# Four moves at once in the first group of a fused attention, Fourier-mixing and feed-forward kernel: where weight combinations keep their temporaries, a third accumulator bank, statistics by chunk, and keys loaded ahead of values

## The chip, the cores and the metric

The kernel runs on one core of one Trainium2 chip. The metric is the device time of one launch, in microseconds (us), as the median of several runs. Before the change it was 1323.78 us (three runs, 1320.86 to 1325.08). A difference under 2% counts as "the same".

## The reference

Eight batches of 576 tokens, 8 heads of 64. Efficient attention (queries softmaxed along the head, keys along the sequence, k-transpose times v first), then a two-dimensional Fourier mix whose real part is added, a normalisation, and a feed-forward layer of 512 to 2048 to 512:

```python
q_s = softmax(q, axis=-1); k_s = softmax(k, axis=sequence)
x   = q_s @ (k_s^T @ v)                       # per head, then heads side by side
u   = x + real(fft(fft(x, axis=sequence), axis=model))
un  = (u - mean(u)) / sqrt(var(u) + 1e-6)
out = u + max(un @ w_ch1, 0) @ w_ch2          # w_ch1: 512 x 2048, w_ch2: 2048 x 512
```

## The kernel before

Each batch is a group. Group 0 takes the weights as they are ("plain": 16 blocks of the first layer, then the second layer). From group 1 on both layers run as a seven-product (Strassen) scheme with weights combined in advance. The combinations are made once, beside group 0's second layer: eight combinations for the first weight (layer 0) and eight for the second (layer 1), each of four additions that GpSimd and VectorE share. The sums go into temporaries, from there by stores to device memory (w1s, w2s), and come back as loads, numbered 15, 16, ... for group 1.

```python
# the tile "words" and the tile "unT" (normalised rows, transposed) share one buffer: same tag, bufs=1
self.words = self.work.tile([P, 7, 2, HD], F32, tag="unT", name="words", bufs=1)
unT        = self.work.tile([P, 7, 2, HD], F32, tag="unT", name="unT", bufs=1)

def combine(self, layer, p):
    w = self.w2sb if layer else self.w1sb
    t = [self.words[:, 4 + (2 * (NP * layer + p) + i) % 3] for i in range(2)]   # three places in turn
    ...                                                          # four additions into t
    nc.sync.dma_start(to[:, first], one)                         # two stores straight from w
    nc.sync.dma_start(to[:, second], two)
    for i in range(2):
        nc.sync.dma_start(to[:, 3 + 2 * i:5 + 2 * i], t[i])      # two stores of temporaries

def up(f):                                                       # a block of group 0's first layer
    n = ("ba", "bb")[f % 2]                                      # two accumulator banks
    ph = self.ps.tile([P, 512], F32, tag=n, name=n)
    ...                                                          # four matmuls into ph
    nc.scalar.activation(h[:, f, :], ph[:], ACT.Relu)            # gives the bank back

# main loop, group 0, beside the second layer
combine = [lambda l=l, p=p: blk.combine(l, p) for l in range(2) for p in range(NP)]
combine[NP:NP] = [lambda i=i: blk.load(15 + i) for i in range(4)]
side += norm(1)
merged(down, mixed(side, combine))
```

The words tile also receives the last three pieces of the second weight ("the fetch of the last pieces"), and since it shares unT's buffer it does not exist before the first layer has read unT for the last time. A scheduler orders the instructions of every engine when the program is built, by what it thinks is ready; the program's text gives priorities, not the order. And in the built program every transfer is issued by SyncE in order, and each waits for the one eight before it to have landed, because eight completion counters are used in turn.

## Time and profile before

| stage of the profiled run (TensorE) | us |
|---|---|
| start to first query transposes | 27.72 |
| to the first block of the first layer | 58.99 |
| first layer of group 0, 16 blocks | 72.42 |
| second layer, with attention and mixing of group 1 between | 91.91 |
| hole: to VectorE's first addition for group 1's products | 29.13 |
| from there to the end | 1039.1 |

The stage borders are start times of rows of the timeline: the first transposes of queries, the first matmul of the first layer (L608 before, L617 after), the first of the second layer (L617, L626), the end of its last, and VectorE's first addition into the tile u (L647, L656). The lines behind this table stand in the prediction. A row reads: start, duration, engine, source line, operation, output<-inputs, form, count, and in brackets the idle time before it and who ended it.

### The profile page before, as it was taken

To read this page: it belongs to the slowest core of one execution; us is meant where nothing else is said; L and a number is where in the kernel's file an instruction comes from. 1 tells how busy PE (TensorE), PEld (TensorE's weight loads), DVE (VectorE), ACT (ScalarE), POOL (GpSimd) and SP (SyncE) were. 2 spreads that over 40 slices of the span, in tenths; PEclk is the share of its full clock that TensorE was granted. 3 is DMA by queue.
4 is the path that set the end of the run, shared out by engine and by line. 5 is a ranking of instruction groups with operands and counts; after the bars stand their busy time and mean duration, and the time that the engine had idled before them with its cause. 6 is when DMAs were issued, how large, how long until landed. Compare 5 with 4: busy or idle time off the path is not lost.

```text
span 1319.3 us, 14360 instructions
## 1 busy us (share of the span) xinstructions
PE 1215.1 (92%) x5484; PEld 949.4 (72%) x5484; DVE 541.7 (41%) x1143; ACT 320.6 (24%) x585; POOL 380.3 (29%) x317
## 2 busy tenths in 40 slices
PE   6858999679999989998999899999999999999797
PEld 4433354368778767887788778877788778888686
DVE  5877272566332551447134613371334143202211
ACT  3555231034111420134113311241124101201100
POOL 2554252133401350016302630253023301421230
PEclk9779999889999999999999999999999999999899
DMA  8446363355225532354335432642353325353342
GB/s 257 140 156 237 117 219 116 122 173 182 111 92 155 192 128 96 126 197 148 130 130 170 170 128 92 201 179 100 116 183 119 117 92 165 142 188 121 148 183 63
DMA packets 90964, 194.52 MB, mean 147 GB/s; under 512 B 22736, under 2 KB 56272, under 8 KB 83728
## 3 DMA queue, kind: packets, MB, share of 16 engines
q1 hardware_dynamic: 89288, 192.82, 42.3%
q8 instruction: 43, 0.70, 0.2%
q10 hardware_dynamic: 1608, 0.79, 0.2%
q14 instruction: 25, 0.20, 0.0%
HBM read 168.94 MB, written 28.84 MB: 150 GB/s over the span
## 4 chain that ended last, share of the span: by engine, by line
PE 68%; DVE 5%; POOL 3%; DMA 1%; issue 1%; ACT 1%; POOLq 0%; DVEq 0%
PE bb L715 13%; PE bb L679 11%; PE bc L715 9%; PE ba L715 8%; PE ba L679 7%; PE bc L679 6%; PE acc L493 4%; PE acc L377 2%; PE acc L518 1%; PE tr L580 1%; PE acc L515 1%; DMA big<-w1s 1%; PE tr L364 1%; POOL q L409 1%; DVE qrec L412 1%
## 5 line engine op out<-in xcount | busy, mean ns | idle before, releaser
L679 PE MATMUL bb<-unT,big 128*128 128x256 f32 x768 | 191.8, 390 | 20.6 <-DVE u L647 15.7
L679 PEld LDWEIGHTS bb<-unT,big 128*128 128x128 f32 x768 | 145.9, 194 | 48.0 <-DVE u L647 18.9
L715 PE MATMUL bb<-big 128*128 128x256 f32 x768 | 177.1, 381 | 0.0
L715 PEld LDWEIGHTS bb<-big 128*128 128x128 f32 x768 | 143.4, 190 | 25.4 <-issue 6.7
L679 PE MATMUL ba<-unT,big 128*128 128x256 f32 x512 | 127.7, 389 | 7.8 <-DMA big<-w1s 7.8
L679 PE MATMUL bc<-unT,big 128*128 128x256 f32 x512 | 125.5, 382 | 0.0
L265 POOL TENSOR_TENSOR big<-big 128x512 f32<-128x512 f32 x32 | 40.5, 1267 | 274.5 <-ACT big L691 274.5
L715 PE MATMUL bc<-big 128*128 128x256 f32 x512 | 117.8, 382 | 0.5 <-DVE x L738 0.5
L715 PE MATMUL ba<-big 128*128 128x256 f32 x512 | 113.7, 379 | 0.0
L679 PEld LDWEIGHTS ba<-unT,big 128*128 128x128 f32 x512 | 97.3, 195 | 21.9 <-issue 8.7
L715 PEld LDWEIGHTS bc<-big 128*128 128x128 f32 x512 | 95.1, 190 | 17.8 <-issue 5.1
L715 PEld LDWEIGHTS ba<-big 128*128 128x128 f32 x512 | 97.1, 190 | 13.9 <-issue 0.8
L679 PEld LDWEIGHTS bc<-unT,big 128*128 128x128 f32 x512 | 94.4, 190 | 13.9 <-DVE big L690 1.3
L691 ACT ACTIVATE big<-big 128x512 f32<-128x512 f32 x96 | 60.4, 630 | 162.9 <-DVE big L690 162.8
L733 POOL TENSOR_TENSOR x<-x,u 128x512 f32<-128x512 f32 x14 | 17.9, 1281 | 230.8 <-DVE u L651 154.5
L493 PE MATMUL acc<-ft,eo 128*128 128x289 f32 (+3 forms) x240 | 76.5, 442 | 1.6 <-POOL eo L477 1.6
L647 DVE TENSOR_TENSOR u<-bb,s 128x512 f32<-128x512 f32 x40 | 27.6, 689 | 102.7 <-PE bb L679 68.4
L493 PEld LDWEIGHTS acc<-ft,eo 128*128 128x128 f32 (+3 forms) x240 | 37.6, 173 | 34.1 <-issue 24.8
L617 PE MATMUL bc<-big 128*128 128x512 f32 x128 | 60.0, 610 | 0.8 <-DVE x L622 0.8
L499 DVE COPY ZT<-acc 128x31 f32<-128x31 f32 x32 | 6.1, 190 | 131.3 <-ACT Z L498 131.3
L259 POOL TENSOR_TENSOR big<-big 128x512 int32<-128x512 int32 x27 | 42.2, 1572 | 52.6 <-DVE big L255 27.5
L690 DVE TENSOR_TENSOR big<-bc,u 128x512 f32<-128x512 f32 x64 | 44.1, 689 | 23.9 <-PE bc L679 23.0
(172 smaller groups left out, 1639.1 us busy)
## 6 DMA issues: line engine op xcount, KB each, us to landing
big<-w1s SPq DMA_DIRECT2D x64, 896.0 KB
big<-w2s SPq DMA_DIRECT2D x56, 1024.0 KB
big<-in_w_dram SPq DMA_DIRECT2D x29, 512.0 KB
k<-in_kT_dram SPq DMA_DIRECT2D x28, 288.0 KB
v<-in_v_dram SPq DMA_DIRECT2D x28, 256.0 KB
q<-in_q_dram SPq DMA_DIRECT2D x28, 256.0 KB
w1s<-words SPq DMA_DIRECT2D x16, 256.0 KB
w2s<-words SPq DMA_DIRECT2D x16, 256.0 KB
```

The source lines that it names most:

```text
L259: nc.gpsimd.tensor_tensor(out=out.bitcast(I32), in0=ti, in1=lo, op=ALU.add)
L265: e1.tensor_tensor(out=to(4), in0=at(2), in1=at(3), op=ALU.add)
L364: nc.tensor.transpose(pt[:, c, :], k[:, c * P:(c + 1) * P], self.ident[:])
L377: nc.tensor.matmul(pk, lhsT=ks[0:n, c, :], rhs=v[0:n, c, :], start=(c == 0), stop=(c == NC - 1))
L493: nc.tensor.matmul(pz, lhsT=eo[c][int(odds)][s, cols], rhs=self.ft[s, 3 * int(odds) + c, :], start=(c == 0), stop=(c == 2 and odds))
L617: nc.tensor.matmul(po[:], lhsT=h[:, f, i * P:(i + 1) * P], rhs=self.w2sb[:, f, :], start=(f == 0), stop=(f == NF - 1))
L647: V.tensor_tensor(out=temp("u2"), in0=box["bb"][:], in1=box["s1"][:], op=ALU.add)
L679: nc.tensor.matmul(bank()[:, i, :], lhsT=w[:, WA_AT[m], k * P:(k + 1) * P], rhs=unT[:, B_AT[m], k, :], start=first and i == 0 and k == 0, ...
L690: V.tensor_tensor(out=hp(i), in0=bank[:], in1=u[:], op=ALU.add)
L691: nc.scalar.activation(hp(i), hp(i), ACT.Relu)
L715: nc.tensor.matmul(bank()[:, i, :], lhsT=h[p][:, A_AT[m], i * P:(i + 1) * P], rhs=w[:, p, :], start=first and i == 0 and p == 0, stop=p == ...
L733: nc.gpsimd.tensor_tensor(out=x, in0=x, in1=t[:, c], op=ALU.add)
```

## The change

Its intent: the combinations' temporaries leave the words tile, so that group 1's unT need not wait for their stores; the other three parts shorten group 0. Source lines move by 6 to 9 (L608 becomes L617, L610 L619, L617 L626, L584 L591, L679 L688).

```diff
@@ first @@
-            if r == 0:
+            if r == 1:
                 load(v ...)                       # values after the second key tile, not the first
@@ combine @@
-        t = [self.words[:, 4 + (2 * (NP * layer + p) + i) % 3] for i in range(2)]
+        pairs = lambda a: a.rearrange("p (s n) -> p s n", s=2)
+        temp = lambda n: self.work.tile([P, 2, HD], F32, tag=n, name=n, bufs=1)[:]
+        if layer == 0 and p > 1:
+            t = [pairs(self.w1sb[:, p - 2 + NP * i, :]) for i in range(2)]
+        elif layer == 0:
+            t = [temp("s1"), temp("u2")] if p == 0 else [temp("u3"), pairs(self.halves()[:, 0:D])]
+        else:
+            t = [pairs(self.w1sb[:, NP + 2 * (p % 2) + i, :]) for i in range(2)]
@@ norm, cut: statistics and square roots of group 0 for chunks (0, 2), then (1, 3) @@
-            for i in range(4):
-                stats(i)
-            scales()
+            for some in ((0, 2), (1, 3)) if g == 0 else (range(4),):
+                for i in some:
+                    stats(i)
+                scales(slice(some[0], 4, some[1] - some[0]))
-        return unT, [all_stats] + pipelined(range(4), [normal, turn]) + [combine]
+        return unT, [all_stats] + pipelined((0, 2, 1, 3), [normal, turn]) + [combine]
@@ plain.up @@
-            n = ("ba", "bb")[f % 2]
+            n = ("ba", "bb", "bc")[f % 3]
@@ main loop @@
-            combine[NP:NP] = [lambda i=i: blk.load(15 + i) for i in range(4)]
+            combine[NP:NP] = [lambda i=i: blk.load(15 + i) for i in range(3)]
+            combine.append(lambda: blk.load(18))
```

More of the change, by code (lines that the diff above doesn't have):

```diff
@@ L565, in stats, with scales @@
             V.bn_aggr(mv[:, i, :], st[:])
-        def scales():
-            nc.scalar.activation(std[:], mv[:, :, 1], ACT.Sqrt, bias=self.eps[:, 0:1])
-            V.reciprocal(std[:], std[:])
+        def scales(s):
+            nc.scalar.activation(std[:, s], mv[:, s, 1], ACT.Sqrt, bias=self.eps[:, 0:1])
+            V.reciprocal(std[:, s], std[:, s])
         def normal(i):
```

## The prediction

> **What bounds the kernel now.** I read the page first: one core, TensorE busy for 92% of the span, so only time in which TensorE stands still or runs at a lower clock can be won. Then the table of stretches of 20 us, to find where that is.
>
> ```profile
> PE 1215.1 (92%) x5484; PEld 949.4 (72%) x5484; DVE 541.7 (41%) x1143; ACT 320.6 (24%) x585; POOL 380.3 (29%) x317
> ```
>
> In the stretches the columns are the stretch, then busy time of TensorE, its weight loads, VectorE, ScalarE, GpSimd, then clock, DMA share, GB/s:
>
> ```profile
> 80.00:100.00 20.00, 14.66 (x37) 7.66 (x38) 12.86 (x26) 8.05 (x13) 15.02 (x8) 0.77 0.57 194
> ...
> 220.00:240.00 20.00, 20.00 (x61) 9.77 (x60) 7.67 (x23) 3.13 (x6) 0.73 (x1) 1.00 0.19 66
> 240.00:260.00 20.00, 11.04 (x32) 4.96 (x30) 8.96 (x23) 0.30 (x1) 2.13 (x3) 0.83 0.32 108
> 260.00:280.00 20.00, 8.23 (x32) 6.52 (x32) 11.28 (x25) 6.88 (x12) 7.01 (x6) 0.66 0.67 200
> ```
>
> From 160 to 250 us TensorE is nearly full, and after 282 us too (longer stretches, from weights to weights, show 90 to 100% busy up to 1204 us). The losses lie before 160 and between 251 and 282. The chain of the page is no help for them: it goes back only to 277 us. So I took the timelines of single engines. The hole in the middle, on TensorE and then on ScalarE:
>
> ```profile
> 247.44 3.60 PE L617 MATMUL bc<-big 128*128 128x512 f32 x8
> 270.47 1.97 PE L580 MATMUL tr<-ident,eo 128*128 128x128 f32 x8 [19.43 <-ACT unT L584]
> 272.23 2.63 PE L679 MATMUL ba<-unT,big 128*128 128x256 f32 x8
> ```
>
> ```profile
> 269.83 1.07 ACT L584 COPY unT<-tr 128x512 f32<-128x512 f32 x2 [3.29 <-DMA w2s<-words]
> ```
>
> TensorE transposes the normalised rows of group 1 and ScalarE copies them to unT. unT shares its one buffer with words, in which the weight combinations keep their temporaries until their stores have landed. The list of waits of 158 to 300 us says the same from the other side:
>
> ```profile
> POOL words L273 <- DMA w2s<-words: 48.0, 3, 30.2
> ...
> PE tr L580 <- ACT unT L584: 19.4, 1, 19.4
> ```
>
> Three temporaries in rotation mean that every combination waits for stores of the one before. Seven of the eight of the second layer were unfinished when VectorE came to an addition that stands before them and waits for TensorE's output until 251.08 us; then they came at one per some 2.4 us, up to 267.3 us. That chain, and not work, is the hole.
>
> Before 160 us the first layer of group 0 (L608) is the place, on TensorE, with ScalarE's line that ends the last stall below it:
>
> ```profile
> 86.71 3.70 PE L608 MATMUL ba<-unT,big 128*128 128x512 f32 x8 [0.68 <-ACT unT L584]
> ...
> 96.23 5.36 PE L608 MATMUL ba<-unT,big 128*128 128x512 f32 x8 [2.39 <-ACT big L610]
> ...
> 119.81 5.37 PE L608 MATMUL bb<-unT,big 128*128 128x512 f32 x8 [2.82 <-ACT big L610]
> 126.82 3.67 PE L608 MATMUL ba<-unT,big 128*128 128x512 f32 x8 [1.64 <-POOL big L259]
> ...
> 143.62 5.37 PE L608 MATMUL ba<-unT,big 128*128 128x512 f32 x8 [2.84 <-ACT big L610]
> ```
>
> ```profile
> 141.78 0.66 ACT L250 ACTIVATE big<-big 128x512 f32<-128x512 f32 x1 [7.22 <-DMA big<-in_w_dram]
> 142.91 0.57 ACT L610 ACTIVATE big<-ba 128x512 f32<-128x512 f32 x1
> ```
>
> A block of the first layer starts every 3.44 us when nothing waits; 16 are 55.0 us, but they took 86.71 to 159.13 = 72.4 us. The banks ba and bb are given back by a Relu (L610) that stands on ScalarE behind conversions of the second weight, and those wait for that weight's loads. The start of the kernel has a wait of its own, on VectorE:
>
> ```profile
> 9.32 0.75 DVE L350 TENSOR_REDUCE km<-big 128x1 f32<-128x576 f32 x1 [3.04 <-DMA big<-in_kT_dram]
> ```
>
> **What the Trainium skill says.** "Perfetto Trace Analysis", section "Optimization Strategy": find the gaps of the contended engine, and which semaphore ends each. That is the reading above. "TensorE: Matmul & The Clock Gate", section "Part 1: The HAM clock gate": the array runs at half clock after some 3.4 us of idleness until it has been busy as long. The trace agrees in kind: a block after a stall took 5.36 us instead of 3.60, the eight passes after the hole 2.63 instead of 1.89, and both stretches show a clock under 1. So a removed stall returns somewhat more than itself. "SBUF — State Buffer", section "Who interferes with whom": GpSimd and VectorE share ports, and a VectorE operation in a two-port mode (tensor_scalar) shuts GpSimd out while it lasts. The trace has a GpSimd addition L259 that took 6.44 us at 84.99, under unbroken VectorE work, against 1.28 elsewhere; this matters for the combinations that move forward. "DMA: Bandwidth & Descriptors", section "Issuing engines are not separate DMA queues": all transfers run on the same 16 engines. So stores moved forward compete with the weight loads; DMA share there is 0.57 to 0.65 (80 to 140 us), which leaves room.
>
> **The change part by part.** The order of instructions in the built changed program tells more than the diff.
>
> (1) Temporaries in places of weights done with. No combination touches words any more; only three loaded pieces of weights do, and their last conversion ends near 177 us. In the built order the combinations of layer 1 (first) move up among the conversions, those of the second all stand before the last output addition, and group 1's statistics, normalisation and copies wait for none. Now the new time line. TensorE ends its second layer at 251.04; one transpose block moves ahead of that (+0.44), one stays behind it (0.44, and about 0.2 latency). Then the first products of group 1. Up to the product at 284.53 there are five groups of eight passes at 1.73: 8.65. So that product starts at 251.04 + 0.44 + 0.44 + 0.2 + 8.65 = 260.8, plus about 0.5 for the wait on the four additions that combine unT (0.69 on VectorE, 1.72 on GpSimd, started after the last copy): 261.3. Gain 284.53 - 261.3 = **23.2 us**, clock loss included. The load put last (18) is issued after the last output addition, near 252.5; 896 KB land some 5 us later by the rate of 200 to 250 GB/s in the windows. It is needed by the second pair, after 262. Hidden.
>
> (2) Keys ahead of values. Key tile 1 (288 KB) lands about 4 us earlier (1.15 MB of values at the 243 GB/s of the first 20 us are no longer ahead of it), and the values land when it did at the latest. But the copy L368 of the first keys' last rows now stands behind the third keys' maximum, which still comes near 10.2, so the first key-value product ends near 12.2, the second starts near 13.9 instead of 16.23. I take **2.2 us**, carried through a start that is bound by this chain.
>
> (3) Statistics by chunk. On VectorE the first reciprocal no longer stands behind two conversion steps (0.41 + 1.28 + 1.41), so normalising starts 2.5 us earlier. ScalarE's copies, however, still come behind the conversion of the second weight's first piece, which lands at 80.8 (relative to the old start). Copies then run 81.5 to 84.3 instead of 83.4 to 86.7: **2.3 us**. The price: conversions of first weights 9 to 15 move behind the normalising, VectorE is then busy without a gap, GpSimd is shut out for longer, and the loads of the second weight that wait for its additions come some 4 us later.
>
> (4) Three banks. Each block waits for the Relu of three blocks before. What sets the end of this layer is the Relu of block 10 at 142.91, behind the load of piece 13. It released block 12; now it releases 13. One block less behind it: **3.4 us**. Parts (2) and (3) reach the end only through the time of this Relu. I follow the chain of pieces 8 to 13 (load 3.4 us, conversion, GpSimd, next load 4.2 us) with the inserted combinations, and get 141.8, so 1.1 us from both together, not 4.5. Layer ends near 154.6 instead of 159.1: **4.5 us** for (2) to (4).
>
> Against it: the 16 stores of temporaries of layer 1 (256 KB each; after 160 us before) now run before about 155, and load 15 (896 KB, 4 us) stands ahead of the last three pieces of weights. The third key tile of group 1 and the last weights come later than TensorE wants them: **-1 us**.
>
> Sum: 23.2 + 4.5 - 1 = 26.7. 1323.8 - 26.7 = **1297.1 us**. From group 1 on the engines' orders are the same in both programs, so nothing else should move.
>
> **Rivals.** First: the unT wait gives way to another. Combinations still wait for stores, now in two alternating pairs of places, and these waits sit in order on VectorE and GpSimd in front of key copies and additions which TensorE needs. For: the old GpSimd waits of 30 us. Against: between 205 and 250 there is little that TensorE needs from GpSimd, and the built order leaves only the end of the last combination after 210. It would give back 5 to 10: 1302 to 1307. Second: the first layer is bound by the loads and conversions of the second weight, whatever the banks. Then (2) to (4) bring nothing or, by the crowd on GpSimd, lose 3: 1301 to 1304. For: every stall there ends with a conversion or a load. Third: stalls of the first layer vanish more fully than I count, with their slow blocks (three times 1.77): then 6 more, 1291.
>
> **Range and chances.** The 23.2 are nearly sure, give or take 1.5; the 3.5 of the rest may be -3 to +9. I give 1290 to 1304. Two per cent is 1297.3, on top of my value, so faster and same are about even: faster 0.5, same 0.49, slower 0.01.
>
> **What would show it.** No TensorE gap over 2 us near 250, and group 1's first product starts within 1.5 us of the end of the second layer; no wait of ScalarE's unT copies on a store. Second key maximum before 6 us. First-layer block 0 starts near 82, the layer ends near 154 to 155, with one stall before block 13. The prediction is wrong if a wait on stores shows up in 160 to 250 on TensorE, if load 18 holds up the second pair, or if the first layer ends at 159 again.

## The result, and the profile after

The changed kernel took 1303.94 us in the median of four runs (1298.75 to 1304.36), beside 1322.32 us for the kernel before (four runs). The ratio is 0.985, with a 95% interval of 0.982 to 0.988, which counts as the same at the limit of 2%. Ratios here are the mean time of one kernel's runs over that of the other's of the same rounds, so they are not quite the ratios of the medians that are quoted. The time lies at the upper end of the predicted range (1290 to 1304), 6.8 us above the predicted 1297.1.

The page after, busy time of each engine, shows the same work in a shorter span (1302.0 us in place of 1319.3):

```profile
PE 1213.9 (93%) x5484; PEld 949.6 (73%) x5484; DVE 542.4 (42%) x1144; ACT 320.5 (25%) x586; POOL 383.4 (29%) x317
```

In the stretches of 20 us (columns as in the prediction), TensorE is now full on both sides of 260, and at full clock:

```profile
80.00:100.00 20.00, 16.62 (x44) 7.66 (x42) 13.40 (x28) 5.98 (x11) 19.10 (x10) 0.94 0.49 153
240.00:260.00 20.00, 20.00 (x70) 11.34 (x69) 11.07 (x26) 6.40 (x10) 1.71 (x1) 1.00 0.34 105
260.00:280.00 20.00, 20.00 (x108) 17.63 (x107) 16.56 (x40) 8.55 (x18) 8.98 (x7) 1.00 0.74 250
```

The hole is gone from TensorE's timeline: the last product of the second layer, the last transposes, and group 1's first product follow each other without a bracket.

```profile
251.78 3.60 PE L626 MATMUL bc<-big 128*128 128x512 f32 x8
255.22 0.60 PE L587 MATMUL tr<-ident,eo 128*128 128x128 f32 x4
255.65 1.89 PE L688 MATMUL ba<-unT,big 128*128 128x256 f32 x8
```

But the second layer ends 4.3 us later than before, 255.38 for 251.04. The first layer starts 3.2 us earlier and ends only 0.8 earlier, and its stalls are longer than they were:

```profile
83.52 3.70 PE L617 MATMUL ba<-unT,big 128*128 128x512 f32 x8 [0.68 <-ACT unT L591]
...
102.66 5.37 PE L617 MATMUL bb<-unT,big 128*128 128x512 f32 x8 [4.28 <-ACT big L619]
...
126.56 5.37 PE L617 MATMUL ba<-unT,big 128*128 128x512 f32 x8 [4.80 <-POOL big L265]
...
142.80 5.37 PE L617 MATMUL ba<-unT,big 128*128 128x512 f32 x8 [3.71 <-ACT big L619]
...
158.30 7.03 PE L626 MATMUL bc<-big 128*128 128x512 f32 x16
...
173.18 2.79 PE L384 MATMUL acc<-v,ks 128*128 128x128 f32 x10 [6.44 <-ACT ks L372]
```

The name POOL L265 in the second bracket gives a hint, and no more than that: the view names the releaser that came last. In the built program this block waits for the Relu (L619) of block 6 and for an old conversion, not for L265; that Relu ended at 126.41, 0.03 us before the addition that the bracket names. But L265 is the first addition of a combination of the first weight, and that it runs inside the first layer is new. Its rows between 80 and 200 us, before and then after (source line, count, shortest/median/longest ns, first to last start):

```profile
L265 POOL TENSOR_TENSOR words<-big x8: 723/758/914, 159.4 to 190.5; 128x256 f32<-128x256 f32 x8
```

```profile
L265 POOL TENSOR_TENSOR big<-big x6: 732/902/1183, 106.2 to 151.6; 128x256 f32<-128x256 f32 x6
L265 POOL TENSOR_TENSOR u<-big x1: 1057/1057/1057, 89.9 to 89.9; 128x256 f32<-128x256 f32 x1
```

Before, no combination could start ahead of 159.4, since their place did not exist until the first layer had ended. After, seven of the eight run in the middle of that layer, and the first just ahead of it, at 76.26. There they share GpSimd with the additions that finish the second weight's conversion (L259) and with the subtraction of the query maxima (L416), and VectorE with the rest of the conversion: in the first layer GpSimd is busy for 49.2 us instead of 31.0, VectorE for 53.9 instead of 36.9. ScalarE, which works in order, waits for that subtraction, and its Relu, which gives the bank back, waits behind it, here before the second stall and before the third:

```profile
122.13 0.63 ACT L417 ACTIVATE q<-q 128x512 f32<-128x512 f32 x1 [7.13 <-POOL q L416]
...
125.83 0.58 ACT L619 ACTIVATE big<-ba 128x512 f32<-128x512 f32 x1
...
141.54 0.63 ACT L417 ACTIVATE q<-q 128x512 f32<-128x512 f32 x1 [6.27 <-POOL q L416]
142.07 0.58 ACT L619 ACTIVATE big<-ba 128x512 f32<-128x512 f32 x1
```

The last of these, at 142.07, starts close to where the prediction put the one that matters (141.8), 0.84 us before its forerunner at 142.91. But it is block 9's and releases block 12 at 142.80, where the prediction had block 10's releasing 13: the layer is one block behind. It falls behind at this very Relu. In e2_no_temps (below), which has the same three banks and no combinations here, block 11 starts at 134.74 and block 12, without a wait, at 138.17; here they start at 135.41 and 142.80. (The first two stalls are another matter: before 102.66 ScalarE waits for loads of the second weight, and block 9 waits in e2_no_temps too, 5.12 us, to start at 125.13.)

The second place is the start of the second layer. The fetch of the last pieces, SyncE's issues before and after:

```profile
159.32 0.81 SPq L236 DMA_DIRECT2D words<-in_w_dram  x2
```

```profile
162.89 0.33 SPq L314 DMA_DIRECT2D big<-w1s  x1
163.32 0.85 SPq L236 DMA_DIRECT2D words<-in_w_dram  x2
```

Before, it was issued 0.2 us after the first layer's end; now it stands 5.0 us behind it, in order behind stores of combinations and load 15. SyncE stands for 3.9 of these 5.0 us in front of load 15 (L314), until a store of the first weight's combinations has landed. The first piece also lands later after its issue, 6.6 us instead of 3.8. The first conversion of these pieces on ScalarE, before and after:

```profile
163.08 0.67 ACT L250 ACTIVATE big<-words 128x512 f32<-128x512 f32 x1 [3.16 <-DMA words<-in_w_dram]
```

```profile
169.95 0.66 ACT L250 ACTIVATE big<-words 128x512 f32<-128x512 f32 x1 [10.85 <-DMA words<-in_w_dram]
```

The Trainium skill, "Perfetto Trace Analysis", section "Tensor Engine Instruction (MATMUL, LD_WEIGHTS)", says that ScalarE, VectorE and GpSimd are "strict FIFO". The trace agrees: the copy of keys L372, ready long before, stands on ScalarE behind that conversion, and TensorE waits 6.44 us for it at 173.18.

By stages, the profiled runs (all in us; every row adds up to its span):

| kernel | start | to layer 1 | first layer | second layer | hole | to the end | span |
|---|---|---|---|---|---|---|---|
| before | 27.72 | 58.99 | 72.42 | 91.91 | 29.13 | 1039.1 | 1319.3 |
| after | 26.79 | 56.73 | 74.78 | 97.08 | 4.67 | 1042.0 | 1302.0 |
| difference | -0.9 | -2.3 | +2.4 | +5.2 | -24.5 | +2.9 | -17.3 |

### The profile page after: what moved, and what is told of

It is laid out like the page before. It is cut to its first block, busy times and chain, and to the rows that moved or that the text cites. A ratio compares the mean times of both kernels' runs of the same rounds, so it can differ in the third digit from the quotient of the medians.

```text
span 1302.0 us, 14354 instructions
## 1 busy us (share of the span) xinstructions
PE 1213.9 (93%) x5484; PEld 949.6 (73%) x5484; DVE 542.4 (42%) x1144; ACT 320.5 (25%) x586; POOL 383.4 (29%) x317
## 4 chain that ended last, share of the span: by engine, by line
PE 74%; DVE 4%; DMA 4%; POOL 3%; issue 1%; ACT 1%; SPq 0%; POOLq 0%; DVEq 0%; ACTq 0%
PE bb L724 13%; PE bb L688 11%; PE bc L724 9%; PE ba L724 9%; PE ba L688 7%; PE bc L688 7%; PE acc L500 4%; PE bc L626 3%; PE acc L384 3%; DMA q<-in_q_dram 2%; DMA big<-w1s 1%; PE acc L525 1%; PE tr L587 1%; PE acc L522 1%; PE tr L371 1%
## 5 line engine op out<-in xcount | busy, mean ns | idle before, releaser
L688 PE MATMUL bb<-unT,big 128*128 128x256 f32 x768 | 192.7, 391 | 18.9 <-DVE u L656 14.7
L688 PEld LDWEIGHTS bb<-unT,big 128*128 128x128 f32 x768 | 146.6, 195 | 46.1 <-DVE u L656 19.5
L724 PEld LDWEIGHTS bb<-big 128*128 128x128 f32 x768 | 143.4, 190 | 25.4 <-issue 6.7
L688 PE MATMUL ba<-unT,big 128*128 128x256 f32 x512 | 127.6, 388 | 7.6 <-DMA big<-w1s 7.6
L688 PE MATMUL bc<-unT,big 128*128 128x256 f32 x512 | 125.2, 381 | 0.0
L265 POOL TENSOR_TENSOR big<-big 128x512 f32<-128x512 f32 (+1 forms) x38 | 46.0, 1211 | 268.3 <-ACT big L700 262.8
L688 PEld LDWEIGHTS ba<-unT,big 128*128 128x128 f32 x512 | 97.3, 195 | 21.9 <-issue 8.6
L724 PEld LDWEIGHTS bc<-big 128*128 128x128 f32 x512 | 95.1, 190 | 17.8 <-issue 5.1
L688 PEld LDWEIGHTS bc<-unT,big 128*128 128x128 f32 x512 | 94.6, 190 | 13.1 <-DVE big L699 0.6
L656 DVE TENSOR_TENSOR u<-bb,s 128x512 f32<-128x512 f32 x40 | 27.6, 689 | 101.6 <-PE bb L688 67.3
L273 POOL TENSOR_TENSOR unT<-unT 128x512 f32<-128x512 f32 x8 | 14.2, 1770 | 180.6 <-DVE unT L272 180.6
L626 PE MATMUL bc<-big 128*128 128x512 f32 x128 | 58.9, 600 | 0.3 <-DVE x L631 0.3
L259 POOL TENSOR_TENSOR big<-big 128x512 int32<-128x512 int32 x27 | 45.0, 1674 | 41.2 <-DVE big L255 21.5
```

Of the source, the lines that this page charges most:

```text
L259: nc.gpsimd.tensor_tensor(out=out.bitcast(I32), in0=ti, in1=lo, op=ALU.add)
L265: e1.tensor_tensor(out=to(4), in0=at(2), in1=at(3), op=ALU.add)
L273: e2.tensor_tensor(out=to(1), in0=at(3), in1=at(1), op=ALU.subtract)
L626: nc.tensor.matmul(po[:], lhsT=h[:, f, i * P:(i + 1) * P], rhs=self.w2sb[:, f, :], start=(f == 0), stop=(f == NF - 1))
L656: V.tensor_tensor(out=temp("u2"), in0=box["bb"][:], in1=box["s1"][:], op=ALU.add)
L688: nc.tensor.matmul(bank()[:, i, :], lhsT=w[:, WA_AT[m], k * P:(k + 1) * P], rhs=unT[:, B_AT[m], k, :], start=first and i == 0 and k == 0, ...
```

## The experiments

Twelve kernels were run, in five rounds each, with the kernel before beside them on the same chip. The stage table of their profiled runs, in the order told below:

| label | what it is | start | to layer 1 | first layer | second layer | hole | to the end | median (runs) | ratio to before, 95% |
|---|---|---|---|---|---|---|---|---|---|
| e1_only_temps | temporaries alone | 25.40 | 61.79 | 74.35 | 97.25 | 5.00 | 1039.7 | 1306.65 (4) | 0.9876 (0.9856 to 0.9897) |
| e2_no_temps | the other three alone | 27.38 | 57.03 | 69.41 | 91.80 | 29.22 | 1040.4 | 1316.69 (6) | 0.9950 (0.9931 to 0.9969) |
| e3_load15_late | whole, load 15 late | 23.85 | 57.05 | 74.32 | 98.65 | 4.67 | 1043.5 | 1303.80 (5) | 0.9855 (0.9833 to 0.9878) |
| e4_stats_whole | whole, statistics as before | 26.38 | 60.21 | 72.69 | 99.62 | 5.00 | 1041.2 | 1306.64 (6) | 0.9873 (0.9849 to 0.9898) |
| e5_second_temps_all | whole, first weight's temporaries back | 24.42 | 57.43 | 68.99 | 93.67 | 6.17 | 1056.9 | 1309.44 (6) | 0.9912 (0.9886 to 0.9939) |
| e6_second_temps_only | only the second weight's moved | 27.04 | 59.35 | 71.98 | 93.63 | 6.18 | 1054.4 | 1316.47 (6) | 0.9967 (0.9939 to 0.9996) |
| e7_two_banks | whole, two banks | 24.48 | 56.92 | 79.35 | 95.13 | 4.67 | 1041.4 | 1300.28 (6) | 0.9851 (0.9823 to 0.9878) |
| e8_values_first | whole, values first | 23.61 | 56.96 | 74.57 | 96.88 | 4.67 | 1041.0 | 1303.57 (6) | 0.9871 (0.9841 to 0.9902) |
| e9_held_and_spread | combinations held back, then all at once | 27.00 | 58.42 | 68.53 | 101.56 | 5.53 | 1043.5 | 1304.41 (4) | 0.9874 (0.9859 to 0.9889) |
| e10_whole_again | the change, unchanged | 24.54 | 58.60 | 74.23 | 96.78 | 4.66 | 1040.5 | 1302.85 (4) | 0.9867 (0.9849 to 0.9886) |
| e11_paced | held back and paced | 26.17 | 57.19 | 68.99 | 99.49 | 4.66 | 1044.8 | 1303.27 (6) | 0.9852 (0.9824 to 0.9881) |
| e12_paced_four | the same, four pairs of places | 24.19 | 57.16 | 69.05 | 99.89 | 9.16 | 1042.2 | 1309.10 (6) | 0.9910 (0.9876 to 0.9943) |

### The temporaries alone (e1_only_temps)

The `combine` and main-loop hunks of the change, applied to the kernel before; nothing else.

> The kernel before with the first part of the change alone: the temporaries of the combinations out of the tile of the last weight pieces, and load 18 behind the combinations. Theory A (the traces' reading: this part carries all of the gain; the first layer's end came only 0.8 us earlier, so the other three parts are worth 0 to 1 us): the median is that of the whole change, 1303 to 1305 us against about 1322, and group 1's first product follows the last product of group 0 within 1.5 us. Theory B (the prediction's sum with one term mis-sized: the three small parts do bring 4.5 us, and the loss of 4.5 us behind load 15 eats it): without them it is 1307 to 1309. Theory C (the three small parts do harm, because the unbroken VectorE work of the new order starves GpSimd at 81 us and delays the loads of the second weight): 1300 to 1302. In all three the words fetch stands behind load 15 as in the whole change, so the TensorE stall before the second k times v of group 1 is there, 5 to 7 us.

It took 1306.65 us, between theories A and B. The stages say more than the sum: the hole shrinks from 29.13 to 5.00 us, a gain of 24.1, and at the same time the first layer is 1.9 us longer and the second 5.3 us longer than before. So the first part brings its gain whole and pays for it in both layers by itself.

### The other three parts alone (e2_no_temps)

```diff
-        t = [... pairs(self.w1sb ...) ...]
+        t = [self.words[:, 4 + (2 * (NP * layer + p) + i) % 3] for i in range(2)]
-            combine[NP:NP] = [... for i in range(3)]; combine.append(lambda: blk.load(18))
+            combine[NP:NP] = [lambda i=i: blk.load(15 + i) for i in range(4)]
```

> The changed kernel with the first part undone: temporaries back in the tile of the last weight pieces, load 18 back; keys first, chunk statistics and three banks stay. Theory A: 1321 to 1323, as before, with the hole of some 24 us before group 1 there again, and the first layer's end within 1 us of the kernel before's. Theory B: 1317 to 1318. Theory C: 1323 to 1326. If the hole is set by store landings that do not move with the first layer's end, small gains in the first layer vanish in the hole and all theories give 1321 to 1323; then the trace's first-layer end decides: 158 to 159 for A, 154 to 156 for B, later than 159 for C.

It took 1316.69 us, 5.9 less than the kernel before, and its first layer ends at 153.82:

```profile
84.41 6.24 PE L610 MATMUL ba<-unT,big 128*128 128x512 f32 x8 [0.68 <-ACT unT L584]
...
138.17 3.60 PE L610 MATMUL ba<-unT,big 128*128 128x512 f32 x8
143.44 3.67 PE L610 MATMUL bb<-unT,big 128*128 128x512 f32 x8 [1.67 <-ACT big L612]
...
265.34 1.97 PE L580 MATMUL tr<-ident,eo 128*128 128x128 f32 x8 [19.72 <-ACT unT L584]
```

That is close to theory B, and theory A (the three small parts bring 0 to 1) falls. The first layer took 69.41 us instead of 72.42, and its end moved by 5.3 us, where the prediction had 4.5. The hole stays (19.72 us of wait on TensorE, 29.22 to the first addition), and it moved along with the layers rather than swallowing their gain. Alone, then, the three small parts do what was predicted, and the temporaries bring their gain at the hole but cost some 7 us in the two layers. In the first layer the halves also cost each other: -3.0 us for the small parts and +1.9 for the temporaries would make 71.3 us, and together it is 74.78.

### Load 15 out of the way (e3_load15_late)

```diff
-            combine[NP:NP] = [lambda i=i: blk.load(15 + i) for i in range(3)]
-            combine.append(lambda: blk.load(18))
+            combine[NP:NP] = [lambda i=i: blk.load(15 + i) for i in range(1, 3)]
+            combine += [lambda i=i: blk.load(i) for i in (15, 18)]
```

> The whole change, and load 15 issued with load 18 behind all combinations. Theory A on the second layer (the 4.5 us lost there come because load 15, 896 KB, waits on SP for the last store of the first layer's temporaries and the fetch of the last weight pieces stands behind it in order and shares its bandwidth): the fetch issues at 159 to 160 instead of 163.3, the stall of TensorE before the second k times v shrinks from 6.4 us to under 3, group 1 starts 3 to 5 us earlier, and the end is 1299 to 1301 us. Rival: the second layer is held by the engines' chain of conversions and key copies or by the clock, whatever the fetch: 1303 to 1305, with a stall of 5 to 7 us still. Second rival: load 15, issued near 240, lands too late or pushes the stores and key loads of group 2: later than 1305, with a wait for a load of the weights at group 1's first product.

A miss: 1303.80 us, a second layer of 98.65. The fetch was issued 5.3 us after the first layer's end (155.22), as late as in the changed kernel (5.0), and the stall was there:

```profile
160.54 0.97 SPq L236 DMA_DIRECT2D words<-in_w_dram  x2
```

```profile
169.21 2.08 PE L384 MATMUL acc<-v,ks 128*128 128x128 f32 x8 [5.55 <-ACT ks L372]
```

With load 15 gone, stores of the second weight's combinations moved up in the built order and took its place: ten issues of w2s stores stand ahead of the fetch, the last held until 159.80, where the changed kernel has seven. Load 15 by itself is not the cause; what stood in its place did the same.

### Statistics in one piece again (e4_stats_whole)

```diff
-            for some in ((0, 2), (1, 3)) if g == 0 else (range(4),):
+            for some in (range(4),):
-        ... pipelined((0, 2, 1, 3), [normal, turn]) ...
+        ... pipelined(range(4), [normal, turn]) ...
```

> The whole change with the statistics of group 0 in one piece again and the normalising in the old order 0, 1, 2, 3 (the third part undone alone). Theory A: 1303 to 1305; the first layer starts some 2 us later than 83.5 and ends at 158 to 160. Theory B (the part is worth its 2.3 us): 1305.5 to 1307. Theory C (the part starves GpSimd and delays the loads of the second weight by some us): 1300 to 1302.5, with the seven loads of the second weight issued at 80 to 86 us instead of 89.8 and the waits of ScalarE for them near 93 gone.

It took 1306.64 us, 2.7 to 3.8 more than the two medians of the whole change, as theory B has it. But its runs spread from 1302.25 to 1311.62, and its ratio to the kernel before (0.9873) lies within the intervals of both (0.985 and 0.9867), so the times do not decide. The stage in question, from the query transposes to the first layer, is 60.21 us here and 61.79 with the temporaries alone, which also lacks this part; over the four profiles without chunk statistics it is 59.0 to 61.8 (mean 60.1), over the ten with them 56.7 to 58.6 (mean 57.3). So the part brings 2 to 3 us there. Counted from the start of the kernel, the first layer begins at 86.4 to 87.2 us in the four, whose starts took 25.4 to 27.7, and at 80.6 to 85.4 in the ten, mostly in the order of their starts (23.6 to 27.4): in these profiles a quick start reaches the layer only with this part.

### Only the second weight's temporaries moved (e5_second_temps_all, e6_second_temps_only)

```diff
-        if layer == 0 and p > 1: ...
-        elif layer == 0: ...
+        if layer == 0:
+            t = [self.words[:, 4 + (2 * p + i) % 3] for i in range(2)]
         else:
             t = [pairs(self.w1sb[:, NP + 2 * (p % 2) + i, :]) for i in range(2)]
```

The first applies this to the changed kernel, the second to the kernel before (with load 18 behind the combinations).

> The whole change, but the combinations of the first weight keep their temporaries in the tile of the last weight pieces, as before; only those of the second weight go to places of weights done with. Theory A (what the whole change lost came from the first weight's combinations: freed from that tile, they run inside the first layer on GpSimd and VectorE and their stores stand ahead of the fetch of the last weight pieces; the hole before group 1 was due to the second weight's temporaries alone): the first layer ends at 153 to 155 us as without the first part, the fetch issues within 1 us of it, the second layer takes some 92 us, no wait for a store before group 1's unT copy, group 1's first product at 246 to 249, and the end at 1293 to 1297 us. Rival (the stores of the first weight's combinations alone still hold unT past 250): a hole of 5 us or more stays, 1299 to 1304. Second rival (the loss in the second layer has another cause, such as load 15 and the key loads): second layer 96 or more, 1298 to 1301.

> The kernel before, with nothing but the temporaries of the second weight's combinations moved (and load 18 behind the combinations). Theory A: the first layer ends at 159 as before, the second layer takes some 92 us, the hole of some 24 us goes: 1297 to 1301 us, which is faster than the first part whole alone (1306.65) by 6 to 9 us. Rivals: 1304 to 1308 if the loss has another cause than where the first weight's combinations run.

Up to group 1 theory A is right in every stage: first layer 68.99 and 71.98 us (as without the first part), second layer 93.67 and 93.63, and the hole gone, 6.2 us. In e5_second_temps_all the first addition of group 1 came at 250.68, 9.4 us before that of the changed kernel. The times are nevertheless misses, 1309.44 and 1316.47, because the stretch from there to the end took 1056.9 and 1054.4 us instead of some 1041. In e5_second_temps_all SyncE is held up by stores that stand in front of group 2's keys, and TensorE then waits for the keys. (The first row merges four issues: the second went out at 250.45, 24.5 us after the first.)

```profile
225.50 27.04 SPq L301 DMA_DIRECT2D w2s<-big  x4
```

```profile
269.77 1.12 PE L368 MATMUL tr<-ident,k 128*128 128x128 f32 x4 [8.53 <-ACT k L357]
```

These stores wait for additions of the second weight's combinations, which the scheduler had now put behind group 1's normalising (GpSimd idles from 199.1 to 246.4 and makes them from 248.1 on). The keys, which follow in order, were issued at 264.21; in the changed kernel at 239.83. The gain was made and handed back 20 us later: with the shorter waits that follow, TensorE stands for 12.2 us between 261 and 300 us. e6_second_temps_only shows the same wait for keys, 8.33 us.

### Two banks, and values first (e7_two_banks, e8_values_first)

```diff
-            n = ("ba", "bb", "bc")[f % 3]
+            n = ("ba", "bb")[f % 2]
```

```diff
-            if r == 1:
+            if r == 0:
```

> The whole change with two banks in the first layer again. Theory A (with the first weight's combinations inside the first layer, the Relu copies come late because ScalarE waits behind conversions and q exponentials that wait for GpSimd and VectorE; a third bank lets TensorE run ahead through some of it): the first layer takes 1 to 3 us longer than 74.8, end 1305 to 1307. Prediction's size for the part (3.4 us): 1307 to 1308. Rival (the banks no longer matter): 1303 to 1304.5.

> The whole change with the values loaded after the first key tile again. Theory A (the start gained 0.9 us at the q transposes instead of 2.2, because the third key tile came 1.1 us later): 1304 to 1305. Prediction's size with all of it reaching the end: 1306. Rival (it gains nothing): 1303 to 1304. Runs of one kernel spread by some 5 us, so only a difference of 2 us or more will be read from the times; otherwise the trace's second key maximum (4.6 against 9.3 us) and q transposes (26.8 against 27.7) decide.

With two banks the first layer takes 79.35 us, 4.6 more than the changed kernel's 74.78, but the second layer is 2 us shorter (95.13), and the timed runs do not show the difference: a median of 1300.28, below that of the whole change and below all that was expected, with a ratio (0.9851) like that of the change (0.985). What the third bank is worth in the layer is shown; that it is worth anything at the end, beside these temporaries, is not.

Values first took 1303.57 us, between the two medians of the whole change, and its start was the shortest of all profiles (23.61 us). A start is best compared at one clock: where all the products of keys and values ran slowly, it took 27.04 and 27.72 us with values first (e6_second_temps_only, before) and 26.79, 27.00 and 27.38 with keys first (after, e9_held_and_spread, e2_no_temps). Loading keys ahead of values brings nothing that these runs can show.

### Combinations held back until the layer is over (e9_held_and_spread), and the change again (e10_whole_again)

```diff
-            t = [temp("s1"), temp("u2")] if p == 0 else [temp("u3"), pairs(self.halves()[:, 0:D])]
+            t = [self.words[:, 4], self.words[:, 5]] if p == 0 else [self.words[:, 6], temp("u3")]
-            t = [pairs(self.w1sb[:, NP + 2 * (p % 2) + i, :]) for i in range(2)]
+            t = [pairs(self.w1sb[:, (12 + 2 * p) % NF + i, :]) for i in range(2)]
-            combine[NP:NP] = [... for i in range(3)]; combine.append(lambda: blk.load(18))
+            combine += [lambda i=i: blk.load(15 + i) for i in range(4)]
```

> The whole change with three edits that follow from the runs so far. The first two combinations of the first weight take their temporaries from the tile of the last weight pieces (and u3), which is not free before the first layer ends, so that the combinations after them, which write over places whose stores come later, cannot start inside the first layer. The combinations of the second weight take eight different pairs of places, all of the first weight's, so that none of them waits for another's store. The four loads for group 1 follow all combinations. Theory A (the two losses of the whole change come from the first weight's combinations running inside the first layer and standing ahead of the fetch; the loss of the run with only the second weight's temporaries moved came from its late stores ahead of group 2's key loads): first layer 69 to 70 us, second layer 92 to 95, under 1.5 us to the first product, from there to the end 1040 to 1043: 1292 to 1296 us, 0.978 to 0.981 of before. Rival (the loss of that run after group 1's start has another cause and stays): 1304 to 1310. Second rival (the loads for group 1, now behind 16 more stores, come late): a wait of TensorE for a weight load at group 1's first products, 1297 to 1303.

> The changed kernel again, unchanged, on the same chip as the run above: how far its stages repeat. Expected: 1301 to 1305 us; first layer 74 to 76 us and second layer 96 to 98 in its profile, as the first time; the time up to the first q transposes somewhere in 23.5 to 27.5 us (the profiles so far fall on 23.6 to 24.5 or on 25.4 to 27.7 whatever the kernel) and the stretch from group 1's first addition to the end somewhere in 1039 to 1044. If these two vary while the edits stand still, a loss of 2.9 us in that stretch is none of the change's.

The held version does for the first layer what theory A says, 68.53 us, and the fetch goes out 0.2 us after its end:

```profile
154.14 0.81 SPq L236 DMA_DIRECT2D words<-in_w_dram  x2
```

```profile
173.41 0.79 PE L384 MATMUL acc<-v,ks 64*128 64x128 f32 x2 [10.13 <-DVE ks L375]
```

Still it is a miss, 1304.41 us. With places enough for all of them, the eight combinations follow each other without a pause from 154.19 on, and VectorE works through fifteen of their additions and two conversions before it comes to L375, the copy of the first keys' last rows, at 173.08. TensorE waits 10.13 us for that. VectorE's additions are slower here, too: beside GpSimd's additions most of them take 0.93 to 0.95 us, against 0.41 when GpSimd stands still (172.14). The stretch to the end (1043.5) did not show the late keys again. So an early fetch by itself does not give the short second layer; what else the two engines have in front of them counts as well.

The whole change run again took 1302.85 us. Its layers repeat within 0.6 us (74.23 and 96.78), and the two stretches that were to be watched vary: 24.54 against 26.79 us at the start, 1040.5 against 1042.0 to the end. The start differs mostly because the same rows of ten products of keys and values ran at different speeds, on TensorE in the first profile of the change and then in the second:

```profile
19.50 2.80 PE L384 MATMUL acc<-big,ks 128*128 128x128 f32 x10 [0.52 <-ACT ks L372]
```

```profile
20.15 1.57 PE L384 MATMUL acc<-big,ks 128*128 128x128 f32 x10 [0.52 <-ACT ks L372]
```

The Trainium skill, "TensorE: Matmul & The Clock Gate", section "Part 1: The HAM clock gate", says that the window in which activity is judged is free-running, so that the same kernel leaves the slow clock after a different number of matmuls from run to run. The trace agrees: 2.80 and 1.57 us for the same row.

### Paced (e11_paced, e12_paced_four)

Both keep the first weight's temporaries in the words tile, three places in turn, as in e5_second_temps_all. The second weight's get sixteen different places in the first and four pairs in turn in the second, and loads follow later.

```diff
 # e11_paced, against e5_second_temps_all
-            t = [pairs(self.w1sb[:, NP + 2 * (p % 2) + i, :]) for i in range(2)]
+            t = [pairs(self.w1sb[:, p + NP * i, :]) for i in range(2)]
-            combine[NP:NP] = [... for i in range(3)]; combine.append(lambda: blk.load(18))
+            combine += [lambda i=i: blk.load(15 + i) for i in range(4)]
 # e12_paced_four, against e5_second_temps_all
-            t = [pairs(self.w1sb[:, NP + 2 * (p % 2) + i, :]) for i in range(2)]
+            t = [pairs(self.w1sb[:, NP // 2 + 2 * (p % 4) + i, :]) for i in range(2)]
-            combine[NP:NP] = [... for i in range(3)]; combine.append(lambda: blk.load(18))
+            combine[NP:NP] = [lambda i=i: blk.load(15 + i) for i in range(2)]
+            combine += [lambda i=i: blk.load(i) for i in (17, 18)]
-            side += norm(1)
-            merged(down, mixed(side, combine))
+            merged(down, mixed(side, combine) + norm(1))
```

> The whole change, with the first weight's combinations in the tile of the last weight pieces as in the run of 1309 us (three places there, so that each waits for the stores of one before: they are paced), and those of the second weight in sixteen different places, each in the two that its namesake of the first weight has been read from and stored; the four loads for group 1 follow all combinations. Theory A (what cost the held-back version its 10 us was eight combinations at once on VectorE and GpSimd ahead of the copy of keys; what cost the version with only the second weight's temporaries moved its 15 us was their late run, after the normalising, with group 2's keys behind their stores): first layer 68 to 70 us, second layer 92 to 95, first product within 1.5 us, from group 1's first addition to the end 1040 to 1044: 1291 to 1296 us, 0.977 to 0.981 of before. Rival (work on VectorE and GpSimd beside the first key tiles costs the second layer wherever it comes from): second layer 97 to 101, 1297 to 1303. Second rival (the stores end so late that group 2's keys are late again): 1303 or more.

> The paced version again (first weight's combinations in the tile of the last weight pieces), but the second weight's use four pairs of places in turn instead of eight, so that in the built order the last ones move behind group 1's query work, one of them behind the normalising; and the normalising follows all combinations in program order. Theory A (the paced version's second layer of 99.5 us instead of 93.7 comes from the second weight's combinations on VectorE and GpSimd beside the key and query chains): second layer 94 to 97, first layer 69, group 1's first product within 1.5 us, from group 1's first addition to the end 1040 to 1046 with a wait of up to 4 us for keys if the last combination's stores hold them: 1294 to 1300 us. Rival (the loss in the second layer is due to stores and loads on the queue, not to the engines): 98 to 100, 1301 to 1305. Second rival (the one late combination brings back the late keys): the stretch to the end 1048 or more, 1303 to 1309.

The first layer is 69.0 us in both, as expected; the second is 99.49 and 99.89 instead of 92 to 97. In e11_paced TensorE waits for 6.9 us in the second layer (2.7 before), by the sum of the brackets in its timeline, and has a mean granted clock of 0.95 there instead of 0.98; its own work takes 92.6 us instead of 89.2. The hole does not come back in the first (4.66), and the late keys do not either, but the stretch to the end is the longest of the versions without them (1044.8). At 1303.27 us it is as fast as the changed kernel and no faster. e12_paced_four is inconclusive: its six runs spread from 1303.08 to 1317.62, the profile belongs to one of the fastest, and it has 9.16 us of the hole again. Neither beats the changed kernel, and no version tried beats it by more than the spread of the runs.

## Why the prediction was right or wrong

The range held the time by 0.06 us at its upper end, while its middle value was 6.8 us off. That it held at all is luck in part, since the losses in the two layers could as well have come out a little larger. One of its own signs of being wrong nearly came true: the first layer ended at 158.30, where it had named 159. The steps fared differently.

**The hole, 23.2 us: right.** From the end of the second layer to group 1's first addition the change took 24.5 us away, and 24.1 by itself. The product that started at 284.53 starts at 264.52; it was predicted for 261.3, and the 3.2 us between are more than made up of the later end of the second layer (255.38 for 251.04, where the prediction had 251.04 unchanged in this step). No copy to unT waits for a store any more. One reading beside it was too generous: the slow blocks that the prediction shows for the clock followed stalls of 2.39 to 2.84 us, shorter than the 3.4 us that it quotes, so these rows do not confirm that figure.

**Keys ahead of values, 2.2 us: wrong.** The second key maximum came at 4.63 us, before 6 as predicted, but the third, which the working took to stay near 10.2, came at 11.28, behind a landing:

```profile
4.63 0.74 DVE L357 TENSOR_REDUCE km<-big 128x1 f32<-128x576 f32 x1
...
11.28 0.75 DVE L357 TENSOR_REDUCE km<-big 128x1 f32<-128x576 f32 x1 [4.16 <-DMA big<-in_kT_dram]
```

The copy L375 waits behind it, as the working said it would, and now a microsecond later. The start gained 0.9 us in the first profile; with the part undone it was shorter still. What the start varies by, 23.6 to 27.7 us over all profiles, is for the most part the speed of these products: each of the last two rows of ten took either 1.57 or 2.80 us, up to 2.5 us in all. The rest goes with when the first keys and values landed.

**Statistics by chunk, 2.3 us: right in kind and size** (2 to 3 us before the first layer). The price that the prediction named was paid too: under unbroken VectorE work one GpSimd addition that takes 1.28 us elsewhere took seven times as long, and the seven loads of the second weight behind it were issued from 89.84 on. Before, two of them went out at 80.52 and five from 91.46 on, so only the first two were late:

```profile
80.82 8.99 POOL L259 TENSOR_TENSOR big<-big 128x512 int32<-128x512 int32 x1 [2.90 <-ACT eo L250]
```

**Three banks, 3.4 us, and 4.5 us for (2) to (4) at the first layer's end: right without the moved temporaries, wrong with them.** Alone the three parts brought the layer's end to 153.82 (predicted 154.6). In the whole change it ended at 158.30. The bank's own 3.4 us were not measured without the moved temporaries; with them it is worth 4.6 us in the layer.

**The step that failed is the last term, "-1 us".** The prediction saw in the built order that "the combinations of layer 1 (first) move up among the conversions" and that the stores of their temporaries run before 155. It charged them with the delay of late weights at the second layer's start, and took the first layer's own chain to reach 141.8 "with the inserted combinations". In its place the runs show two losses. The first layer is 74.2 to 74.8 us long with three banks whenever the first weight's combinations run inside it (after, e3_load15_late, e8_values_first, e10_whole_again; e4_stats_whole, with the old statistics, 72.7), and 68.5 to 69.4 whenever they do not (e2_no_temps, e5_second_temps_all, e9_held_and_spread, e11_paced, e12_paced_four). That is 5 us, and it eats the gain of the three small parts there. The second layer is 91.8 to 93.7 us in the four versions in which the first weight's combinations are paced by three places in the words tile and the second weight's come late, and 95.1 to 101.6 in all others; 5.2 us in the change (0.44 of it a transpose block that moved ahead, as predicted), where the prediction had 1. TensorE's waits there grew from 2.7 to 6.8 us. Summed for the profiled runs: predicted 23.2 + 4.5 - 1 = 26.7, measured 24.5 + 0.8 - 5.2 - 2.9 = 17.2, or 17.3 with the digits that were rounded away.

**"From group 1 on nothing else should move": not shown to be wrong.** The stretch to the end was 2.9 us longer in the first profile and 1.4 in the second, but it varies between 1039.1 and 1044.8 us over versions without late keys. Those with the hole in place or with the temporaries alone lie at the low end, and I have no run that separates this from chance; it stays open. So does the split of the second layer's 5 us between the queue (late fetch) and the two small engines (combinations ahead of key copies). e3_load15_late shows that load 15 by itself is not the cause, and e9_held_and_spread that a timely fetch is not enough, yet no run has both a timely fetch and free engines except those whose combinations come late.

**The rivals.** The first (the wait gives way to another, in order, in front of key copies, 1302 to 1307) named the time and the place. It described waits in alternating places on VectorE and GpSimd. Such waits stand in the trace (VectorE 5.17 us at 163.55, GpSimd 6.24 us at 165.20, both for w2s stores), but the stall at 173.18 ends with a copy on ScalarE that the late fetch holds up; how much those waits add to the 5 us is not shown. The second (the first layer gains nothing, by the crowd on GpSimd, 1301 to 1304) had the size: the layer ended only 0.8 us earlier. Its reason, that the layer is bound by loads and conversions whatever the banks, does not hold: without the moved temporaries the end came 5.3 us earlier, and with two banks the layer is 4.6 us longer. Each was set against the main line alone; they came together.

## What to carry to other kernels

A temporary's place is also a brake: work that loses a wait moves forward as far as the scheduler lets it, and one should ask which stage it lands in and what is bound there, not only what it no longer blocks. Two parts of a change that each gain by themselves can cost each other (here 3.4 us in the first layer), so predict them together, stage by stage, and undo each of them in turn. And when stage lengths repeat within 0.6 us while whole runs spread by 5, read the stages.

## What the Trainium skill lacked or had wrong

- "DMA: Bandwidth & Descriptors", the section on issuing engines that the prediction cites, says of the time on the issuing sequencer that it "is usually small relative to the DMA itself". One engine issues everything in order, and what it stands waiting for is not small: 24.5 us in front of the stores ahead of group 2's keys in e5_second_temps_all, and 3.9 us in front of load 15, ahead of the fetch, in the changed kernel. The section does not warn of it.
- "SBUF — State Buffer", the section on interference that the prediction cites, gives the rule that VectorE can shut GpSimd out, and names one measurement of a slowed GpSimd, 1.5 times. Here one addition took 8.99 us under unbroken VectorE work and 1.28 us elsewhere, seven times as long.
- "TensorE: Matmul & The Clock Gate", Part 1, is right that the moment of the change to full clock varies from run to run. It calls the ramp under 1% of a typical kernel. Here two rows of products at the start took 2.5 us more or less by it, 0.2% of the span, which is as much as the second or the third part of the change was to bring: small for a model, too large for a comparison of small parts by their times.
